# Numerators added by transfers, scores in four quarters, and GpSimd's arithmetic moved to VectorE and ScalarE, in a fused attention and feed-forward kernel

## The chip, the cores and the metric

The kernel runs on one core of a Trainium2 chip. The metric is the device time of one execution in microseconds (us). TensorE is called PE here, its weight load PEld, VectorE DVE, ScalarE ACT, GpSimd POOL, and SyncE, which issues the DMA transfers, SP, as the profile names them.

## What is computed

The reference, cut to what matters, with four batches, 8 heads, 576 positions, head size 64, window 64 (2304 tokens of 512 numbers in all):

```python
scores = q @ k.T / 8, masked to 0 <= i - j < 64
attn = softmax(scores);  x = attn @ v           # 2304 x 512
h = x @ w_in                                    # 2304 x 2048
P = a0 + a1*h + a2*h*h + a3*h*h*h
Q = 1 + |b0|*|h| + |b1|*h*h
x = (P / (Q + 1e-6)) @ w_out                    # 2304 x 512
out = ((x @ w1) * (x @ w2)) @ w3 @ wo2          # 2304 x 512
```

## The kernel before

All products of large matrices are made of three fp32r products of high and low parts (`TERMS`). Each weight tile is converted on DVE and ACT into such a pair (`conv`, lines 431 to 512: three shifts, a high part on ACT, a low part on DVE).

The 2304 tokens are cut into five blocks (`TOKENS`, line 30: two of 384, three of 512). A block has two units for the attention (`US`), of 3 windows of 64 queries (192 tokens) or 4 (256 tokens). A step is one unit and one pair of heads; there are 40 steps, treated in pairs (`attn`, lines 536 to 680). A step multiplies queries by keys into `sp` (`S_`, line 609), one window at a time: in the first four units (`THIN`) as two 64x64 products, one for each head, in the others as one 128x128 product with a query tile in which zeros keep the heads apart. Then follow the masked minimum on DVE (`tr`), the exponential on ACT (`e`), the sum plus 1e-9 on POOL (`rs`, line 557), its reciprocal on DVE (`rc`), the normalisation (`nm`, line 627: ACT, POOL or DVE, as the planner chooses), a transposition on PE (`T`), a copy on ACT (`ac`), and the product with the values (`O`). From step 24 on the probabilities go through a transfer within SBUF before the transposition (`mv`, tile `tq`). The output of the attention is split into the pair `xh`, `xl`.

The hidden layer (`chunks`, lines 685 to 829) takes two tiles of 128 of the 2048 hidden numbers at a time, called a pair here; a turn is one block and half of the hidden numbers, four pairs, and there are ten turns (`TURNS`, line 307): first blocks 0, 1, 2 with the first half, then 2, 1, 0 with the second, then 3, 4, 4, 3. For a pair PE computes `hp` (`H_`), ACT and DVE form the rational function, and PE multiplies the result `g` with `w_out` into `acc` (`D_`). The denominator is `Q`, `ln`, `ex`. The numerator comes in two ways. Where `estrin` holds (line 697, five of the ten turns), ACT makes a square `h2`, a linear term `u` and a second linear term `bl` from PSUM; DVE multiplies `u` by `h2` (`us`) and adds `bl` (`p`). In the other turns DVE reads PSUM four times for each pair (`uh`, `v`). Then DVE makes the high part of the quotient (`hi`), and by `w`, `d` and `lo` its low part. `lo` may run on DVE or POOL (line 818). The tiles `u`, `qa`, `g` have two buffers, `bl`, `h2`, `r` one.

After the hidden layer come the product of w3 and wo2 (`w_prod`, line 948), the two products of the second layer in Strassen's form (`p_`, line 1093), and the last product (`result`, line 1220).

The order of the instructions on every engine is fixed when the program is built: `Plan.order` (lines 97 to 241) books each operation with a duration on its engine, a tail (time until others may use its result) and a due time, walks through a list schedule with noise of a fixed seed on the due times, and the instructions are issued in that order. Engines take their queues in order and wait on semaphores.

Of the kernel before, what the change touches and what calls it, by code (L numbers as in the profile page):

```python
# [20 lines left out]
P = 128  # L21
# [8 lines left out]
TOKENS = (384, 384, 512, 512, 512)  # L30
# [7 lines left out]
NU = len(US)  # L38
NF = FF // P
# [26 lines left out]
class Plan:  # L66
# [30 lines left out]
    def order(self, rounds=16):  # L97
# [125 lines left out]
        rng = Random(67)  # L223
# [21 lines left out]
def body(ctx: ExitStack, tc: tile.TileContext, qkv, kv0, qk0, w_in, w_out, a, b, w1, w2, w3t, wo2, out):  # L245
# [21 lines left out]
    nc.gpsimd.memset(cq, QC)  # L267
    a0, a1, a2, a3 = (ca[:, i:i + 1] for i in range(4))
# [49 lines left out]
    MM = [{384: TMM, 512: TWM}[t] for t in TOKENS]  # L318
# [4 lines left out]
    TS, TT, TO, TOO = 0.67, 0.33, (0.71, 0.42), 1.9  # L323
# [25 lines left out]
    for t in range(-2 * NP - 1, NI + 1):  # L349
        scale[0] = 2.9 / (TS + TT + TO[0]) if t < 0 else 1.2 if t < 2 * NP * 2 else 1.0  # L350
# [185 lines left out]
    def attn(pair):  # L536
# [13 lines left out]

        def rows(f):
            return y["st"][:, 2 * NW * f:2 * NW * f + 2 * NW]
# [4 lines left out]
        def rs(_):  # L557
            nc.gpsimd.tensor_scalar(out=rows(2), in0=rows(1), scalar1=1e-9, scalar2=1.0, op0=ADD, op1=MUL)
# [4 lines left out]
        def O(k, y=y):  # L563
            if k == 0:
                y["op"] = psum.tile([P, 2, U], F32, tag="at", bufs=2, name="op")
            for w in range(NW):
                for h in (slice(0, 64), slice(64, P)):
                    nc.tensor.matmul(y["op"][h, k, w * W_:(w + 1) * W_], y["v", k][:, w, h], y["ac", k][:, w, h], start=True, stop=True)  # L568
            if u % 2 == 0 and k == 0 and y is units[u][0]:
                xh[j], xl[j] = xtiles(j, "x")  # L570

# [11 lines left out]
        def step(k):  # L583
# [5 lines left out]
            def load(_):  # L589
                x["k"] = ap_.tile([P, KB * W_], F32, tag="k", bufs=rings["k"], name="k")[:, 0:KU]  # L590
                if i < THIN:
                    if k == 0:
                        y["q"] = ap_.tile([P, 2 * UM], F32, tag="q", bufs=rings["q"], name="q")[:, 0:2 * U]
                        nc.sync.dma_start(out=y["q"], in_=qk0[u, p0 // 2])
                    x["q"] = y["q"].rearrange("d (k w n) -> d k w n", k=2, w=NW)[:, k]
                    nc.sync.dma_start(out=x["k"], in_=kv0[u, p, :, 0:KU])
                    return
                q = ap_.tile([P, 2 * UM], F32, tag="q", bufs=rings["q"], name="q")[:, 0:2 * U]
                x["q"] = q.rearrange("d (w n) -> d w n", w=NW)
                nc.sync.dma_start(out=q, in_=qkv[u - THIN // NP, p, :, 0:2 * U])  # L600
                nc.sync.dma_start(out=x["k"], in_=qkv[u - THIN // NP, p, :, 2 * U:2 * U + KU])

            def loadv(_):
                y["v", k] = ap_.tile([P, NWM, P], F32, tag="v", bufs=rings["v"], name="v")[:, 0:NW]
                v = kv0[u, p, :, U + W_:] if i < THIN else qkv[u - THIN // NP, p, :, 2 * U + KB * W_:]
# [3 lines left out]
            def S_(_):  # L609
                x["sp"] = sp = psum.tile([P, NW, P], F32, tag=tags[0], bufs=rings[tags[0]], name="sp")  # L610
                x["sm"] = ap_.tile([P, NWM, P], F32, tag="sm", bufs=rings["sm"], name="sm")[:, 0:NW]
                if k == 0:
                    y["st"] = ap_.tile([P, 8 * NWM], F32, tag="st", bufs=rings["st"], name="st")
# [38 lines left out]
            kb_, vb, qb, mb, sp, tp = ("k", i), ("v", i), ("q", i0 if i < THIN else i), ("sm", i), (tags[0], ("S", i)), (tags[1], ("T", i))  # L652
            thin = i < THIN
            op(("load", i), (("D", (0.48 if k else 1.12) if thin else 1.1 * wide),), load, after=[("load", i0)] if thin and k else (), new=(kb_,) if thin and k else (kb_, qb), uses=(qb,) if thin and k else (), tail=3.0)
            op(("loadv", i), (("D", 0.66 * wide),), loadv, after=(("load", i),), new=(vb,), tail=3.0)
            pe(("S", i), S_, TS * wide, after=[("load", i)] + [("S", i - 1)] * k, new=(sp, mb) if k else (sp, mb, sb), uses=(kb_, qb, sb) if k else (kb_, qb))
            for m in range(NW):
                op(("tr", i, m), (("V", 0.21),), lambda _, m=m: tr(m), after=(("S", i),), uses=(sp, mb, sb))
# [5 lines left out]
            pe(("T", i), T, 0.068 * NW if moved else TT * wide, after=[("mv", i)] if moved else [("nm", i)], new=(tp,), uses=(("tq", i),) if moved else (mb,))  # L664
# [6 lines left out]
        op(("rs", i0), (("P", 0.12),), rs, after=[("e", i0 + k, m) for k in range(2) for m in range(NW)], uses=(sb,))  # L671
# [686 lines left out]
```

## Time and profile before

| | before |
|---|---|
| median of 3 runs | 804.54 us (804.3 to 804.63) |
| profiled execution, device time | 805.03 us |
| its span | 803.3 us |
| PE busy | 782.0 us (97%) |
| PEld busy | 716.3 us (89%) |
| DVE busy | 729.7 us (91%) |
| ACT busy | 542.2 us (67%) |
| POOL busy | 50.5 us (6%) |
| DMA queue of SP | 168.85 MB, 60.5% of 16 engines' span |

The busy time of an engine is the time in which at least one of its instructions ran. Matmuls are pipelined and their ends are modelled, so that how many follow each other in a stretch says more than their durations.

### The profile page before, as it was taken

To read this page: it belongs to the slowest core of one execution; us is meant where nothing else is said; L and a number is where in the kernel's file an instruction comes from. 1 tells how busy PE (TensorE), PEld (TensorE's weight loads), DVE (VectorE), ACT (ScalarE), POOL (GpSimd) and SP (SyncE) were. 2 spreads that over 40 slices of the span, in tenths; PEclk is the share of its full clock that TensorE was granted. 3 is DMA by queue.
4 is the path that set the end of the run, shared out by engine and by line. 5 is a ranking of instruction groups with operands and counts; after the bars stand their busy time and mean duration, and the time that the engine had idled before them with its cause. 6 is when DMAs were issued, how large, how long until landed. Compare 5 with 4: busy or idle time off the path is not lost.

```text
span 803.3 us, 13413 instructions
## 1 busy us (share of the span) xinstructions
PE 782.0 (97%) x4728; PEld 716.3 (89%) x4728; DVE 729.7 (91%) x1361; ACT 542.2 (67%) x1131; POOL 50.5 (6%) x67
## 2 busy tenths in 40 slices
PE   5889999999999999999999999999999999999998
PEld 4679999888899999888888888889999999999998
DVE  6999999999999999999999999999998698847854
ACT  5888998859898988665677772377555447445434
POOL 1112112101100101200100000000000000000000
PEclk9899999999999999999999999999999999999999
DMA  8798884511657755537883365968898676136402
GB/s 292 249 334 305 293 278 157 186 54 65 207 185 282 273 191 203 202 133 236 323 282 143 117 221 183 313 249 292 307 305 282 210 283 195 42 133 222 145 1 78
DMA packets 66403, 169.70 MB, mean 211 GB/s; under 512 B 7456, under 2 KB 24864, under 8 KB 66336
## 3 DMA queue, kind: packets, MB, share of 16 engines
q1 hardware_dynamic: 66336, 168.85, 60.5%
q8 instruction: 37, 0.61, 0.3%
q14 instruction: 30, 0.25, 0.1%
HBM read 123.21 MB, written 41.42 MB: 205 GB/s over the span
## 4 chain that ended last, share of the span: by engine, by line
PE 83%; DVE 12%; DMA 2%; ACT 1%; issue 1%; POOL 0%; SPq 0%; POOLq 0%; DVEq 0%; ACTq 0%
PE acc L781 22%; PE hp L703 20%; PE pb L1093 9%; PE pa L1093 6%; PE pc L1093 6%; PE wp L948 5%; PE pb L1220 5%; PE pc L1220 3%; PE pa L1220 3%; PE sp L616 2%; DVE sm L619 2%; DVE wt L456 1%; DVE wt L453 1%; DVE wc L466 1%; PE op L568 1%; DMA cb<-in_b 1%
## 5 line engine op out<-in xcount | busy, mean ns | idle before, releaser
L703 PE MATMUL hp<-x,wc 128*128 128x512 f32 (+1 forms) x960 | 213.8, 371 | 3.6 <-DVE u L731 3.2
L781 PE MATMUL acc<-g,wc 128*128 128x512 f32 (+1 forms) x960 | 213.1, 370 | 0.0
L703 PEld LDWEIGHTS hp<-x,wc 128*128 128x128 f32 x960 | 173.7, 188 | 27.8 <-DVE u L731 4.2
L781 PEld LDWEIGHTS acc<-g,wc 128*128 128x128 f32 x960 | 173.9, 188 | 22.9 <-issue 0.3
L1093 PE MATMUL pb<-xb,wc 128*128 128x384 f32 x432 | 83.8, 334 | 0.0
L1093 PEld LDWEIGHTS pb<-xb,wc 128*128 128x128 f32 x432 | 75.7, 188 | 0.0
L744 ACT ACTIVATE r<-qa,cq 128x1024 f32<-128x1024 f32 (+1 forms) x40 | 42.8, 1069 | 37.8 <-DVE g L775 21.3
L625 ACT ACTIVATE sm<-sm,st 128x128 f32<-128x128 f32 x144 | 56.1, 395 | 17.3 <-DVE st L619 17.1
L720 ACT ACTIVATE qa<-hp,cb 128x512 f32<-128x512 f32 (+1 forms) x80 | 51.7, 647 | 19.3 <-PE hp L703 19.0
L725 ACT ACTIVATE u<-hp,ca 128x512 f32<-128x512 f32 (+1 forms) x80 | 59.5, 745 | 1.7 <-PE hp L703 1.3
L1093 PE MATMUL pa<-xb,wc 128*128 128x384 f32 x288 | 57.2, 335 | 0.0
L1182 ACT ACTIVATE rt<-prod 128x768 fp32r<-128x768 f32 x42 | 35.6, 847 | 31.9 <-PE pb L1220 13.3
L1093 PE MATMUL pc<-xb,wc 128*128 128x384 f32 x288 | 56.7, 334 | 0.0
L1185 DVE TENSOR_TENSOR rt<-prod,rt 128x768 fp32r<-128x768 f32 x42 | 40.1, 956 | 15.4 <-ACT rt L1182 14.9
L616 PE MATMUL sp<-k,q 64*64 64x128 f32 (+1 forms) x384 | 43.2, 311 | 10.2 <-DMA k<-in_kv 7.2
L463 ACT ACTIVATE wc<-wt 128x512 fp32r<-128x512 f32 x48 | 30.2, 633 | 32.7 <-DVE wt L456 29.0
L1093 PEld LDWEIGHTS pa<-xb,wc 128*128 128x128 f32 x288 | 50.6, 188 | 0.3 <-DMA wc<-kw 0.2
L453 DVE SCALAR_TENSOR_TENSOR wt<-ws,wt 128x512 uint32<-128x512 uint32 x72 | 50.4, 702 | 0.3
L1093 PEld LDWEIGHTS pc<-xb,wc 128*128 128x128 f32 x288 | 50.5, 188 | 0.0
L456 DVE SCALAR_TENSOR_TENSOR wt<-ws,wt 128x512 uint32<-128x512 uint32 x72 | 49.9, 695 | 0.3
L616 PEld LDWEIGHTS sp<-k,q 64*64 64x64 f32 (+1 forms) x384 | 37.9, 182 | 13.7 <-DMA k<-in_kv 4.0
L715 ACT ACTIVATE h<-hp 128x512 f32<-128x512 f32 (+1 forms) x80 | 44.3, 553 | 8.2 <-PE hp L703 7.1
(90 smaller groups left out, 1368.4 us busy)
## 6 DMA issues: line engine op xcount, KB each, us to landing
wc<-kw SPq DMA_DIRECT2D x48, 512.0 KB, 5.4
bs<-kb SPq DMA_DIRECT2D x24, 512.0 KB, 4.5
ws<-in_w_in SPq DMA_DIRECT2D x16, 512.0 KB, 6.1
ws<-in_w_out SPq DMA_DIRECT2D x16, 512.0 KB, 4.2
ws<-in_w SPq DMA_DIRECT2D x16, 512.0 KB, 4.3
kw<-ws SPq DMA_DIRECT2D x16, 512.0 KB, 3.5
ws<-in_w3t SPq DMA_DIRECT2D x16, 512.0 KB, 4.8
wsum<-wsum SPq DMA_DIRECT2D x16, 512.0 KB, 6.1
```

The lines of the kernel that those rows point to most:

```text
L453: stt(out=x["b"], in0=x["st"][:, :, 0], scalar=29, in1=x["b"], op0=ALU.logical_shift_right, op1=ALU.bitwise_or)
L456: stt(out=x["b"], in0=x["st"][:, :, 1], scalar=0xC0000000, in1=x["b"], op0=ALU.bitwise_and, op1=ALU.bitwise_or)
L616: nc.tensor.matmul(sp[h, w, :], x["q"][h, w], x["k"][h, kat[w] * W_:kat[w] * W_ + P], start=True, stop=True)
L625: act(x["sm"][:, m, :], x["sm"][:, m, :], AF.Exp, bias=col(0, k, m), scale=-1.0, accum_out=col(1, k, m))
L703: nc.tensor.matmul(x["hp", m], wf_(win, f0 + m)[:, s_, kk * P:(kk + 1) * P], (xh, xl)[m_][xk][:, kk, :], start=(kk == 0 and i == 0), stop= ...
L715: act(x["h2"][:, m, :], x["hp", m], AF.Square)
L720: act(x["qa"][:, m, :], x["hp", m], AF.Abs, scale=b0)
L725: act(x["u"][:, m, :], x["hp", m], AF.Identity, scale=a3, bias=a2)
L744: act(x["r"], x["qa"], AF.Ln, bias=cq)
L781: nc.tensor.matmul(accs[j, part, n], wf_(wout, f0 + m)[:, s_, n * P:(n + 1) * P], x["g"][:, m_, m, :], start=(first and i == 0), stop=(las ...
L1093: nc.tensor.matmul(x[m], sws[u, n, i0][:, s_, (c0 + k) * P:(c0 + k + 1) * P], t[:, m_, k, :], start=(first and k == 0 and i == 0), stop=(k ...
L1220: nc.tensor.matmul(x[m, n], w[:, s_, (c + n) * P:(c + n + 1) * P], rts[u, b, r][:, m_, k, :], start=(first and r == 0 and k == 0 and i == ...
```

## The change

- The order of the blocks becomes 384, 512, 384, 512, 512, and the pairs of steps stand at other places between the pairs of the hidden layer (`AT`).
- `S_` is one operation for both steps of a pair, in all units with 64x64 products: for each window, both steps and both heads. The first step writes head 0 to the upper half of its `sp` and head 1 to the lower, the second step the other way round, so the four products of a window and a pair use four different quarters of PE. `O` reads the halves of the second step swapped. It waits for both key tiles. The queries come without the zeros, one transfer for each pair of steps, in all units.
- `estrin` holds in all turns but the first. The addition `p` is a transfer within SBUF that adds its source `bl` to its target `u`, issued by POOL, booked as 1.5 us (at 384 tokens) on the DMA queue and a tail of 3.5.
- `rs` runs on DVE or ACT, `nm` on DVE or ACT, `lo` on DVE alone.
- Booked times, seed, and the due times of the first conversions change.

The diff, cut to its core:

```diff
-TOKENS = (384, 384, 512, 512, 512)
+TOKENS = (384, 512, 384, 512, 512)
...
+THINU = NU
...
-        rng = Random(67)
+        rng = Random(57)
...
+    tiny = pers.tile([P, 1], F32, name="tiny")
+    nc.gpsimd.memset(tiny, 1e-9)
...
-        AT[((-8, -6, -4, -2), (0, 1, 2, 3), (4, 5, 6, 6), (16, 18, 19, 20), (22, 24, 25, 26))[j][r // 2]].append(i)
+        AT[((-8, -6, -4, -2), (0, 1, 2, 2), (4, 5, 6, 6), (16, 18, 19, 20), (21, 23, 25, 26))[j][r // 2]].append(i)
...
-    TS, TT, TO, TOO = 0.67, 0.33, (0.71, 0.42), 1.9
+    TS, TT, TO, TOO = .72, 0.33, (0.71, 0.42), 1.9
...
-        if 0 <= i < NS:
+        if 0 <= i < NS and (what != "S" or i % 2 == 0):
...
-        scale[0] = 2.9 / (TS + TT + TO[0]) if t < 0 else 1.2 if t < 2 * NP * 2 else 1.0
+        scale[0] = 3.2 / (TS + TT + TO[0]) if t < 0 else 1.2 if t < 2 * NP * 2 else 1.0
...
-        def rs(_):
-            nc.gpsimd.tensor_scalar(out=rows(2), in0=rows(1), scalar1=1e-9, scalar2=1.0, op0=ADD, op1=MUL)
+        def rs(e):
+            if e == "A":
+                act(rows(2), rows(1), AF.Identity, bias=tiny)
+            else:
+                dve.tensor_scalar(out=rows(2), in0=rows(1), scalar1=1e-9, scalar2=1.0, op0=ADD, op1=MUL)
...
+        def S_(_):
+            for k in range(2):
+                y["place", k]()
+            y["st"] = ap_.tile([P, 8 * NWM], F32, tag="st", bufs=rings["st"], name="st")
+            for w in range(NW):
+                for k in range(2):
+                    for h in range(2):
+                        to = half[h if k == 0 else 1 - h]
+                        nc.tensor.matmul(y["sp", k][to, w, :], y["q", k][half[h], w], y["k", k][half[h], kat[w] * W_:kat[w] * W_ + P], start=True, stop=True)
...
-                for w in range(NW):
-                    for h in (slice(0, 64), slice(64, P)) if i < THIN else (slice(0, P),):
-                        nc.tensor.matmul(sp[h, w, :], x["q"][h, w], x["k"][h, kat[w] * W_:kat[w] * W_ + P], start=True, stop=True)
...
-            op(("nm", i), (("A", 0.32 * NW), ("P", 0.97 * wide), ("V", cost(0.065, 0.40))), nm, port=True, after=(("rc", i0),), uses=(sb, mb))
+            op(("nm", i), (("A", 0.32 * NW), ("V", cost(0.065, 0.40))), nm, port=True, after=(("rc", i0),), uses=(sb, mb))
...
-                op(("mv", i), (("D", 0.66 * wide),), mv, after=[("nm", i)], new=(("tq", i),), uses=(mb,), tail=3.0)
+                op(("mv", i), (("D", 0.66 * wide),), mv, after=[("nm", i)], new=(("tq", i),), uses=(mb,), tail=2.0)
...
-        op(("rs", i0), (("P", 0.12),), rs, after=[("e", i0 + k, m) for k in range(2) for m in range(NW)], uses=(sb,))
+        op(("rs", i0), (("V", 0.09), ("A", 0.2)), rs, after=[("e", i0 + k, m) for k in range(2) for m in range(NW)], uses=(sb,))
...
-        estrin = (j, f0 // HALF) in ((2, 1), (1, 1), (0, 1), (4, 0), (3, 0))
+        estrin = (j, f0 // HALF) in TURNS[1:]
...
         def p(_):
-            dve.tensor_tensor(out=x["u"], in0=x["u"], in1=x["bl"], op=ADD)
+            nc.gpsimd.dma_start(out=x["u"], in_=x["bl"], accum_op=ADD)
...
-            op(("p", c0), (("V", dve_(0.87, 2)),), p, port=True, after=(("us", c0), ("line", c1)), uses=(b["u"], b["bl"]))
+            op(("p", c0), (("D", 1.5 * T_ / 384),), p, tail=3.5, after=(("us", c0), ("line", c1)), uses=(b["u"], b["bl"]))
...
-            engines = (("V", dve_(0.87, 2)),) if whole else (("V", dve_(0.47)), ("P", 0.97 * T_ / 384))
+            engines = (("V", dve_(0.87, 2)),) if whole else (("V", dve_(0.47)),)
...
-    coming = {key: 3.2 * min(n, 12) + 8.5 * max(n - 12, 0) for n, key in enumerate(coming)}
+    coming = {key: 3.2 * min(n, 10) + 8.5 * max(n - 10, 0) for n, key in enumerate(coming)}
```

## Rows read from the trace of the kernel before

**Rows 1.** The page's part 1: busy us (share of span) xinstructions of each engine.

```profile
PE 782.0 (97%) x4728; PEld 716.3 (89%) x4728; DVE 729.7 (91%) x1361; ACT 542.2 (67%) x1131; POOL 50.5 (6%) x67
```

**Rows 2.** Stretches: length, busy of PE, PEld, DVE, ACT, POOL, PEclk, DMA, GB/s.

```profile
0.00:20.00 20.00, 10.64 (x88) 8.74 (x90) 13.70 (x54) 11.55 (x40) 3.37 (x15) 1.00 0.86 292
...
40.00:60.00 20.00, 16.07 (x161) 14.16 (x160) 19.64 (x55) 17.62 (x51) 2.33 (x3) 1.00 0.97 337
60.00:80.00 20.00, 20.00 (x179) 19.02 (x178) 19.79 (x50) 16.44 (x43) 5.01 (x6) 1.00 0.87 301
80.00:100.00 20.00, 20.00 (x162) 19.65 (x163) 20.00 (x55) 20.00 (x63) 2.55 (x5) 1.00 0.86 294
```

**Rows 3.** Timeline of PE, hidden layer at 512: start us, us, line, tile, count.

```profile
165.41 5.60 PE L703 MATMUL hp<-x,wc 128*128 128x512 f32 x24
170.85 4.92 PE L781 MATMUL acc<-g,wc 128*128 128x512 f32 x21
```

**Rows 4.** Timeline of PE around thin scores, value products, and wide scores.

```profile
64.69 1.53 PE L616 MATMUL sp<-k,q 64*64 64x128 f32 x24
66.15 2.36 PE L781 MATMUL acc<-g,wc 128*128 128x384 f32 x12
...
73.86 1.62 PE L568 MATMUL op<-sm,v 128*64 128x64 f32 x48
75.41 1.84 PE L781 MATMUL acc<-g,wc 128*128 128x384 f32 x9
...
255.11 1.95 PE L616 MATMUL sp<-k,q 128*128 128x128 f32 x16
256.82 1.81 PE L781 MATMUL acc<-g,wc 128*128 128x384 f32 x9
```

**Rows 5.** Groups by line and shape: count | busy us, mean ns | idle before, releaser.

```profile
L753 DVE TENSOR_TENSOR u<-u,bl 128x1024 f32<-128x1024 f32 x12 | 14.7, 1222 | 0.1
L753 DVE TENSOR_TENSOR u<-u,bl 128x768 f32<-128x768 f32 x8 | 7.6, 953 | 0.1
L728 DVE TENSOR_TENSOR u<-u,hp 128x512 f32<-128x512 f32 x24 | 15.9, 682 | 1.1 <-ACT u L725 0.9
L731 DVE SCALAR_TENSOR_TENSOR u<-u,ca,hp 128x512 f32<-128x512 f32 x24 | 17.4, 744 | 0.9 <-ACT qa L720 0.8
L775 POOL TENSOR_TENSOR g<-u,r 128x384 fp32r<-128x384 f32 x17 | 19.4, 1159 | 65.7 <-DVE u L770 30.9 <-ACT u L725 13.5 <-ACT sm L650 10.8
L775 POOL TENSOR_TENSOR g<-u,r 128x512 fp32r<-128x512 f32 x11 | 14.9, 1370 | 139.4 <-DVE u L768 59.6 <-PE hp L703 41.7 <-DVE u L770 38.0
L775 DVE TENSOR_TENSOR g<-u,r 128x512 fp32r<-128x512 f32 x37 | 25.0, 707 | 0.0
L736 ACT ACTIVATE bl<-hp,ca 128x512 f32<-128x512 f32 x24 | 19.4, 807 | 0.0
```

**Rows 6.** Timeline of DVE: multiplication and high part of one pair at 512.

```profile
184.03 1.22 DVE L750 TENSOR_TENSOR u<-u,h 128x1024 f32<-128x1024 f32 x1
...
187.50 1.22 DVE L759 TENSOR_TENSOR g<-u,r 128x1024 fp32r<-128x1024 f32 x1
```

**Rows 7.** DMA issues: count, KB each, median us from issue to landing.

```profile
ws<-in_w_in SPq DMA_DIRECT2D x16, 512.0 KB, 6.1
...
kw<-ws SPq DMA_DIRECT2D x16, 512.0 KB, 3.5
...
tq<-sm SPq DMA_DIRECT2D x16, 256.0 KB, 2.5
...
kb<-wt SPq DMA_DIRECT2D x16, 256.0 KB, 2.3
```

**Rows 8.** Groups by line: masked minima of the whole span; conversions up to 80 us.

```profile
L619 DVE CUSTOM_DVE_ANT_0 sm<-sp,mask 128x128 f32<-128x128 f32 x144 | 34.2, 285 | 2.5 <-PE sp L616 2.3
...
L456 DVE SCALAR_TENSOR_TENSOR wt<-ws,wt 128x512 uint32<-128x512 uint32 x14 | 10.1, 722 | 0.1
```

**Rows 9.** Instructions of GpSimd's two lines: count, ns min/median/max, first and last start.

```profile
L775 POOL TENSOR_TENSOR g<-u,r x28: 997/1274/2180, 53.7 to 394.8; 128x384 fp32r<-128x384 f32 x17, 128x512 fp32r<-128x512 f32 x11
...
L558 POOL TENSOR_SCALAR st<-st x20: 196/210/1238, 13.4 to 326.1; 128x8 f32<-128x8 f32 x12, 128x6 f32<-128x6 f32 x8
```

More of the change, by code (lines that the diff above doesn't have):

```diff
@@ L244, in body @@
 @with_exitstack
-def body(ctx: ExitStack, tc: tile.TileContext, qkv, kv0, qk0, w_in, w_out, a, b, w1, w2, w3t, wo2, out):
+def body(ctx: ExitStack, tc: tile.TileContext, kv0, qk0, w_in, w_out, a, b, w1, w2, w3t, wo2, out):
     nc = tc.nc
@@ L549, in attn @@
         y = units.setdefault(u, [{} for _ in range(NP // 2)])[p0 // 2]
+        half = (slice(0, 64), slice(64, P))
         def rows(f):
@@ L598, in load @@
[L598 to L601, printed above, removed]
+                if k == 0:
+                    y["q"] = ap_.tile([P, 2 * UM], F32, tag="q", bufs=rings["q"], name="q")[:, 0:2 * U]
+                    nc.sync.dma_start(out=y["q"].rearrange("d (k n) -> d k n", k=2), in_=qk0[u, p0 // 2].rearrange("d (k n) -> d k n", k=2)[:, :, 0:U])
@@ L603, in loadv, with place @@
+                y["q", k] = y["q"].rearrange("d (k w n) -> d k w n", k=2, w=NW)[:, k]
+                nc.sync.dma_start(out=x["k"], in_=kv0[u, p, :, 0:KU])
+                y["k", k] = x["k"]
             def loadv(_):
                 y["v", k] = ap_.tile([P, NWM, P], F32, tag="v", bufs=rings["v"], name="v")[:, 0:NW]
-                v = kv0[u, p, :, U + W_:] if i < THIN else qkv[u - THIN // NP, p, :, 2 * U + KB * W_:]
+                v = kv0[u, p, :, KU:KU + NW * P]
                 nc.sync.dma_start(out=y["v", k], in_=v.rearrange("r (w d) -> r w d", w=NW))
-            def S_(_):
-                x["sp"] = sp = psum.tile([P, NW, P], F32, tag=tags[0], bufs=rings[tags[0]], name="sp")
+            def place():
+                y["sp", k] = x["sp"] = psum.tile([P, NW, P], F32, tag=tags[0], bufs=rings[tags[0]], name="sp")
@@ L650, in ac @@
                 act(y["ac", k], x["tp"], cp)
-            kb_, vb, qb, mb, sp, tp = ("k", i), ("v", i), ("q", i0 if i < THIN else i), ("sm", i), (tags[0], ("S", i)), (tags[1], ("T", i))
-            thin = i < THIN
-            op(("load", i), (("D", (0.48 if k else 1.12) if thin else 1.1 * wide),), load, after=[("load", i0)] if thin and k else (), new=(kb_,) if thin and k else (kb_, qb), uses=(qb,) if thin and k else (), tail=3.0)
+            kb_, vb, qb, mb, sp, tp = ("k", i), ("v", i), ("q", i0), ("sm", i), (tags[0], ("S", i)), (tags[1], ("T", i))
@@ L655, in step @@
+            thin = True
+            op(("load", i), (("D", (0.48 if k else 1.12) * wide),), load, after=[("load", i0)] if thin and k else (), new=(kb_,) if thin and k else (kb_, qb), uses=(qb,) if thin and k else (), tail=3.0)
             op(("loadv", i), (("D", 0.66 * wide),), loadv, after=(("load", i),), new=(vb,), tail=3.0)
-            pe(("S", i), S_, TS * wide, after=[("load", i)] + [("S", i - 1)] * k, new=(sp, mb) if k else (sp, mb, sb), uses=(kb_, qb, sb) if k else (kb_, qb))
+            if k == 0:
+                sp1, mb1 = (f"acc{(i + 1) % 2}" if early else "at", ("S", i + 1)), ("sm", i + 1)
+                pe(("S", i), S_, TS * wide, after=[("load", i), ("load", i + 1)], new=(sp, mb, sb, sp1, mb1), uses=(kb_, qb, ("k", i + 1)))
@@ L661, in step @@
             moved = i >= MOVED
             if moved:
-                op(("mv", i), (("D", 0.66 * wide),), mv, after=[("nm", i)], new=(("tq", i),), uses=(mb,), tail=3.0)
-            pe(("T", i), T, 0.068 * NW if moved else TT * wide, after=[("mv", i)] if moved else [("nm", i)], new=(tp,), uses=(("tq", i),) if moved else (mb,))
+                op(("mv", i), (("D", 0.66 * wide),), mv, after=[("nm", i)], new=(("tq", i),), uses=(mb,), tail=2.0)
+            pe(("T", i), T, 0.075 * NW if moved else TT * wide, after=[("mv", i)] if moved else [("nm", i)], new=(tp,), uses=(("tq", i),) if moved else (mb,))
@@ L1322, in queries @@
         return out.reshape(NP, P, -1)
[L1324 to L1325 removed]
+    thin = range(THINU)
+    pad = lambda x: np.concatenate([x, np.zeros((NP, P, KB * W_ + NWM * P - x.shape[2]), x.dtype)], axis=2)
+    qk0 = np.stack([pad(queries(u, False))[:, :, :UM] for u in thin])
     return {
[L1327 to L1329 removed]
+        "kv0": np.stack([pad(np.concatenate([keys(u, len(blocks(u)[0])), values(u)], axis=2)) for u in thin]),
+        "qk0": qk0.reshape(THINU, NP // 2, 2, P, -1).transpose(0, 1, 3, 2, 4).reshape(THINU, NP // 2, P, -1),
         "w_in": cols(moe_w_in, NF),
```

24 lines of the change are left out of this document (6 added, 18 removed).

## The prediction

> **What bounds the kernel now.** I read four views in this order: the busy totals, the 20 us stretches, the order of TensorE's matmuls, and the groups by line and shape. The totals [rows 1] name TensorE (PE, 782.0 us of 803.3) with VectorE (DVE, 729.7) close behind. The stretches [rows 2] tell where each of them sets the pace. In the first 60 us PE is busy for 10.64 of 20 and still only 16.07 of 20 at 40 to 60, while DVE rises to 19.64: the start waits for DVE. From 60 us PE shows 20.00 of 20, and DVE 19.79 and 20.00 beside it. A busy PE need not be PE at its peak, so I checked the spacing: 24 hidden-layer matmuls of 512 columns fill 165.41 to 170.85, then the next run begins at once, 227 ns each [rows 3]. The engine is streaming. So past 60 us a microsecond of PE work removed is a microsecond gained, as long as DVE, which is as full, doesn't become later than PE; before 60 us only DVE work counts.
>
> The profiled execution took 805.03 us for its span of 803.3; the median of the runs is 804.54. I take the sum from 804.5, since all steps are differences.
>
> **Scores in quarters.** Before, a pair of thin steps (block of 384, 3 windows) issues 24 products 64x64, two side by side: 64.69 to 66.15 is 1.46 us, 61 ns each [rows 4]. A wide pair (block of 512, 4 windows) issues 16 full products: 255.11 to 256.82 is 1.71 us, 107 ns each [rows 4]. After, both kinds issue 64x64 products, 24 or 32 in a pair, on four quarters in turn. No row shows four quarters. Bounds for one product: 107/4 = 27 ns if they overlap fully, and 61 ns if only two overlap as in the thin row. The nearest row for many small products on PE is the value product: 48 of them from 73.86 to 75.41, 32 ns each [rows 4], where PE already swallows one weight load and one short product every 32 ns. I take 32. A thin pair becomes 24 x 0.0323 = 0.78 us (saves 0.68), a wide pair 32 x 0.0323 = 1.03 (saves 0.68). There are 8 thin and 12 wide pairs before and after. Four thin pairs, those of block 0, lie in the start, where PE waits anyway: worth 0. The rest: 16 x 0.68 = 10.9 us on the path. At 27 ns with all 20 counted it is 12 x 0.85 + 8 x 0.82 = 16.8; at 61 ns it is 12 x (1.71 - 1.95) = -2.9, a loss.
>
> The Trainium skill (TensorEngine Tiling (Array Packing), Restrictions and Gotchas) speaks against it: different row tiles must not write one PSUM bank at the same time. The rows disagree already: the thin products of the kernel before write both halves of one bank from two row halves, and take 61 ns each, where one alone takes the 107 of a 128-column product [rows 4]. By the rule two of them would have to take turns and the change would be worth nothing for thin pairs; I go by the rows.
>
> **DVE's load.** Turns with the split polynomial go from five to nine. The old ones were 12 pairs at 512 and 8 at 384; the new ones are 24 and 12. The addition leaves DVE in the old ones: 12 x 1.222 + 8 x 0.953 = 22.3 us [rows 5]. The 16 pairs that are new lose two products and two fused multiply-adds from PSUM, 2 x (0.682 + 0.744) = 2.85 at 512 [rows 5], and get one multiplication of 1.22 (same shape as the addition): 1.63 x 12 + three quarters of that x 4 = 24.5 us. Against that come 17 and 11 low parts from GpSimd [rows 5], at 0.707 and about 0.53 on DVE: 16.8 us; seven normalisations and twenty little sums are 7 x 0.6 + 20 x 0.2, some 8 us if none goes to ScalarE. Net: DVE is lighter by 22.3 + 24.5 - 16.8 - 8 = 22 us, all of it before 490 us. Since PE has no idle time there, this is worth 0 by itself. It is what lets DVE follow a PE that is 11 us faster, with 22 - 11 = 11 us over, 0.3 us for each of 36 pairs. ScalarE gets 24 and 8 more linear terms at 0.807 and about 0.6 [rows 5], 24 us; at 80 to 100 us it is full too (20.00, [rows 2]), so there the new load can cost a few us; elsewhere I cost it at nothing.
>
> **The adding transfer.** It stands between the multiplication and the high part, which now begins 2.25 us after the multiplication ends (185.25 to 187.50, [rows 6]). No row has an adding transfer or one that GpSimd issues. From below: 256 KB within SBUF land in 2.5 us, 512 KB take 3.5 against 2.3 for 256 KB to memory [rows 7], so 512 KB moved once are 3.7 us. From above: if the target is read too, 1024 KB, 6.1 us, and under load times 6.1/3.5 (the same size with the queue full, [rows 7]): 10.6. I take 6 for 512 KB, near the unloaded row counted twice. The code's planner books 1.5 + 3.5 = 5.0 at 384 tokens and 5.5 at 512, and orders DVE's queue by that; behind the waiting high part stand the next weight conversions and the next pair's denominator, and the output products wait for its low part. With 5.5 booked and 6 needed nothing is lost if DVE has other work in its queue, which its fullness says it mostly has: 0, at worst the rival below. On GpSimd's queue nothing else is left, so its waits hold up nobody. SP loses 12 query transfers of 256 KB.
>
> **The start.** DVE's list up to the end of the first turn (about 90 us) grows: eight low parts and four normalisations of that stretch came from GpSimd, 12 x 0.53 = 6.4; eight sums x 0.2 = 1.6; block 1 now has 4 windows instead of 3 in 8 steps, 8 masked minima x 0.24 [rows 8] = 1.9. Together 9.9 us if all is on the path. Nothing can be dropped: 14 of the 16 conversions that the first turn needs were done by 80 us [rows 8]. But the normalisations may go to ScalarE (2.1), DVE is no longer held by GpSimd (a low part of it takes 1.0 to 2.2 us for the same work, [rows 9]), DVE was idle for 6.3 us of the first 20 [rows 2], and past 60 us the next turn needs less DVE time. Between 0 and +9.9 I take +3.
>
> **Sum.** 804.5 - 10.9 + 3 = 796.6; I say 796.5.
>
> **Rivals.** (1) The transfer is late, slower than before. If it lands later than booked by more than the 0.3 us that DVE has left in a pair, DVE stands still at the high part 36 times, and each us is 36 us. At 1 us too late: 796.5 + 36 x 0.7 = 822. It decides at 0.3 + 8/36 = 0.5 us too late on average. For it: the upper bound of 10.6, and a GpSimd instruction of 0.21 us that once took 1.24 [rows 9], which an issue could suffer as well. Against: DVE's queue holds conversions between the two steps already now [rows 6], so a small delay is filled. The Trainium skill (SBUF — State Buffer, Who interferes with whom) says that GpSimd writes the descriptors of its transfers through the port pair that it shares with VectorE, and that an instruction in a two-port mode keeps it out, while a two-input product doesn't; no row here shows a descriptor written. By that rule only the short shifts (one input) could hold an issue, and the rival would be small.
> (2) Only two quarters overlap: 804.5 + 2.9 + 3 = 810.4. For it: no row has four. Against: 32 ns for the value products.
> (3) The start costs all of its 9.9: 803.5, next to nothing gained. For it: DVE's 19.64 at 40 to 60 us.
> (4) More than forecast: 27 ns, all pairs, no loss at the start: 804.5 - 16.8 = 787.7, and 785 if the earlier scores use DVE's idle time there.
>
> **How the numbers follow.** Forecast 0.60, (1) 0.16, (2) 0.06, (3) 0.10, (4) 0.08. About 0.2% (1.6 us) is what a measurement here can tell from no change; half of (3) falls within it. Faster 0.60 + 0.08 + 0.05 = 0.73, same 0.05, slower 0.22. The range goes from (4)'s 785 to 812, past (2) and a third of the way into (1); what it leaves out is most of (1) and little else.
>
> **What would show it.** Right: a run of 32 score products of a pair in about 1.0 us; PE at 20.00 from about 63 us; DVE near 707 us; the transfer landing in about 6 us with no idle time of DVE before the high part. Wrong: idle time of DVE put down to a DMA on the numerator's tile, PE waiting for low parts past 100 us, score products at 61 ns, or a first full PE stretch that comes at 70 us.

## The result, and the profile after

The changed kernel takes 814.41 us (median of 3 runs, 813.28 to 817.39) against 804.54: a ratio of 1.0131, 95% interval 1.0089 to 1.0173. It is slower, clear of the noise; 796.5 was forecast, and the time lies outside the range of 785 to 812. The profiled execution took 813.28 us, its span 811.5.

The page's part 1 after (busy us, share of the span, instructions), to be read beside [rows 1]:

```profile
PE 777.6 (96%) x4920; PEld 704.6 (87%) x4920; DVE 710.5 (88%) x1350; ACT 552.7 (68%) x1152; POOL 37.5 (5%) x49
```

DVE is 19 us lighter, PE 4.4, and yet the span is 8.2 us longer: both engines wait more. The first place is the start. Stretches (columns as in [rows 2]) of the changed kernel, the first three and one at the end of the hidden layer, and behind them the two of the kernel before that [rows 2] leave out:

```profile
0.00:20.00 20.00, 6.91 (x78) 5.27 (x82) 13.44 (x48) 10.08 (x35) 2.06 (x13) 1.00 0.81 273
20.00:40.00 20.00, 15.87 (x168) 12.38 (x160) 19.84 (x75) 16.00 (x56) 0.00 (x0) 0.91 0.81 278
40.00:60.00 20.00, 14.28 (x123) 13.03 (x124) 16.97 (x46) 17.15 (x54) 0.00 (x0) 0.83 0.84 294
...
480.00:500.00 20.00, 14.69 (x60) 11.76 (x58) 16.50 (x22) 6.46 (x10) 0.86 (x1) 0.91 0.64 216
```

```profile
20.00:40.00 20.00, 16.11 (x176) 12.91 (x173) 18.96 (x61) 16.21 (x58) 3.45 (x6) 0.83 0.76 250
...
480.00:500.00 20.00, 20.00 (x90) 16.57 (x89) 19.93 (x30) 6.93 (x10) 0.00 (x0) 1.00 0.49 174
```

PE is busy for 37.06 us of the first 60, where the kernel before has 10.64 + 16.11 + 16.07 = 42.82. At 480 us it is busy for 14.69 of 20, where it was for 20.00. What PE waited for (us in total, times, longest; "issue" is time in which it waited for nothing that the profile shows), and the waits of DVE and ACT that belong to the transfers (ACT must not overwrite `bl`, which has one buffer, before the transfer has read it):

```profile
PE sp L589 <- DMA k<-in_kv: 7.4, 2, 4.1
PE acc L794 <- DVE g L788: 5.3, 1, 5.3
...
PE hp L716 <- DVE x L600: 3.0, 1, 3.0
PE sp L589 <- issue: 2.9, 1, 2.9
PE hp L716 <- DVE u L744: 2.5, 1, 2.5
...
DVE g L772 <- DMA u<-bl: 9.3, 6, 3.2
...
ACT bl L749 <- DMA u<-bl: 5.7, 5, 2.3
```

Two things came as forecast. A pair of wide scores (timeline of PE: start, us, line, tile, count) starts at 48.66 and ends where the next run begins, at 49.69: 32 products in 1.03 us, 32 ns each, where [rows 4] have 1.71 us for the same scores. And the adding transfers (part 6: count, KB each, median us to landing) take the 5.5 that was estimated as 6:

```profile
48.66 1.10 PE L589 MATMUL sp<-k,q 64*64 64x128 f32 x32
49.69 2.35 PE L716 MATMUL hp<-x,wc 128*128 128x384 f32 x12
...
u<-bl POOLq DMA_DIRECT2D x24, 512.0 KB, 5.5
...
u<-bl POOLq DMA_DIRECT2D x12, 384.0 KB, 4.6
```

To see where time goes I use one figure more: PE's lost time, the length of a stretch less the matmuls that ran in it, each at its spacing in an unbroken run (227 ns at 512 columns as in [rows 3], 173 at 384; scores 107, 61 or 32 and value products 32 as in [rows 4] and above; transpositions 61 and 95). It is good to about 1 us, since records can be missing.

```
PE's lost time, us        0-60 us   60-560 us   median, us
before                      29.4        7.6      804.54
changed                     39.2       18.8      814.41
```

The quarters take 20 pairs x 0.68 = 13.6 us off the work. The lost time grew by 9.8 + 11.2 = 21.0. The difference, +7.4, is most of the 8.2 us by which the two profiled spans differ.

### The profile page after: what moved, and what is told of

The parts are those of the page before. It is cut to its first block, busy times and chain, and to the rows that moved or that the text cites. A ratio compares the mean times of both kernels' runs of the same rounds, so it can differ in the third digit from the quotient of the medians.

```text
span 811.5 us, 13799 instructions
## 1 busy us (share of the span) xinstructions
PE 777.6 (96%) x4920; PEld 704.6 (87%) x4920; DVE 710.5 (88%) x1350; ACT 552.7 (68%) x1152; POOL 37.5 (5%) x49
## 5 line engine op out<-in xcount | busy, mean ns | idle before, releaser
L716 PE MATMUL hp<-x,wc 128*128 128x512 f32 (+1 forms) x960 | 216.9, 376 | 6.5 <-DVE x L600 3.0
L716 PEld LDWEIGHTS hp<-x,wc 128*128 128x128 f32 x960 | 175.9, 191 | 32.2 <-DVE x L600 3.1
L749 ACT ACTIVATE bl<-hp,ca 128x512 f32<-128x512 f32 (+1 forms) x72 | 54.6, 759 | 5.7 <-DMA u<-bl 5.7
L772 DVE TENSOR_TENSOR g<-u,r 128x1024 fp32r<-128x1024 f32 (+1 forms) x36 | 40.8, 1134 | 19.8 <-DMA u<-bl 9.3
L1195 ACT ACTIVATE rt<-prod 128x768 fp32r<-128x768 f32 x42 | 35.5, 846 | 32.3 <-PE pb L1233 10.6
L766 POOL DMA_DIRECT2D u<-bl x36 | 35.4, 983 | 449.0 <-ACT sm L636 113.8
L456 DVE SCALAR_TENSOR_TENSOR wt<-ws,wt 128x512 uint32<-128x512 uint32 x72 | 49.2, 690 | 0.6
```

Of the source, the lines that this page charges most:

```text
L456: stt(out=x["b"], in0=x["st"][:, :, 0], scalar=29, in1=x["b"], op0=ALU.logical_shift_right, op1=ALU.bitwise_or)
L716: nc.tensor.matmul(x["hp", m], wf_(win, f0 + m)[:, s_, kk * P:(kk + 1) * P], (xh, xl)[m_][xk][:, kk, :], start=(kk == 0 and i == 0), stop= ...
L749: act(x["bl"][:, m], x["hp", m], AF.Identity, scale=a1, bias=a0)
L772: dve.tensor_tensor(out=x["g"][:, 0], in0=x["u"], in1=x["r"], op=MUL)
```

## The experiments

Letters: A, the transfers come late; B, the start is late because POOL's work went to DVE and ACT; M, joining two steps delays the start; K, the new sequence of the blocks delays it; P, the random draw of the planner decides. All ratios are to the kernel before on the same chip; it took 804.1 to 804.9 us on each of them, so that times of different experiments compare to about 1 us. "In the same order" means that every engine keeps its queue; "planned anew" means that the planner makes another order.

**e1, the transfers left out,** the changed kernel's order held. The numerators lack their linear part, so it shows time only.

```diff
-            nc.gpsimd.dma_start(out=x["u"], in_=x["bl"], accum_op=ADD)
+            pass
```

> The changed kernel in its own order of instructions, with the 36 adding transfers left out (the numerators lack their linear term). Theory A, the transfers land late and the waits behind them cost the time: the 5.3 us that PE stood still at 483 us, the slow clock behind that and the smaller losses between 60 and 490 us go, some 11 us, so about 803 us. Theory B, the loss is in the start, where VectorE took over GpSimd's work: the transfers begin only at 100 us, so 811 us or more stay.

Measured 804.61, ratio 0.9998 (0.9988 to 1.0007). In this order the transfers cost 9.8 us, 0.27 us for each of 36; the interval of the changed kernel's own ratio makes that good to some 3 us. PE's lost time from 60 to 560 us falls from 18.8 to 10.9, and the wait of 5.3 us shrinks:

```profile
PE acc L794 <- DVE g L788: 0.8, 1, 0.8
```

The start is still as bad (38.1 lost), and that eats what the quarters save: even with the transfers gone nothing is gained on the kernel before.

**e2, the additions on DVE,** in the same order.

```diff
-            nc.gpsimd.dma_start(out=x["u"], in_=x["bl"], accum_op=ADD)
+            dve.tensor_tensor(out=x["u"], in0=x["u"], in1=x["bl"], op=ADD)
```

> The changed kernel in its own order, with each addition as a VectorE instruction in the place where the transfer was issued. VectorE gets 24 x 1.222 + 12 x 0.953 = 40.8 us between 100 and 490 us and had about 29 us idle there. Theory A: the waits go and 12 us of VectorE come, so 812 to 818 us, near the changed kernel. Theory B, and the transfers cost nothing as they are: 826 us or more.

Measured 836.5 (1.0391, 1.0368 to 1.0413). DVE's busy time rises from 710.5 to 747.3, by 36.8 us, and the time by 22.1 over the changed kernel, 31.9 over e1: in this order most of what is added to DVE reaches the end.

**e3, two quarters,** in the same order: both steps of a pair on the two diagonal quarters.

```diff
-                        to = half[h if k == 0 else 1 - h]
+                        to = half[h]
```

> The changed kernel in its own order, with both steps of a pair on the same two diagonal quarters, so that only two products overlap. Wide pairs 32 x 0.061 = 1.95 us for 1.03, thin ones 1.46 for 0.82. If PE sets the pace past the start (both theories) the 9 wide and 4 thin pairs past 60 us cost 9 x 0.92 + 4 x 0.64 = 10.8 us: about 825 us. If the waits behind the transfers set the pace everywhere, PE's work hides in them: 814 to 818 us.

Measured 825.02 (1.0259, 1.0224 to 1.0293): 10.6 us over the changed kernel, near the 10.8 expected for 61 ns a product in place of 32: four quarters do overlap, and in an order that counts on them slower scores are paid in full. This is not the price of the change, which compares 32 products at 32 ns with 16 at 107; that both come to some 11 us is chance.

**e4, the start's small work back on POOL** (low parts of the first turn, the second step's normalisation in block 0, all sums), in the same order.

```diff
+                e = "P" if early and k == 1 else e
...
+            e = "P" if c0 < HALF else e
...
-            if e == "A":
-                act(rows(2), rows(1), AF.Identity, bias=tiny)
-            else:
-                dve.tensor_scalar(...)
+            nc.gpsimd.tensor_scalar(...)
```

> The changed kernel in its own order, with the low parts of the first turn, the second step's normalisation of the first four pairs and all little sums back on GpSimd. Theory B: the start gets back 3 to 6 us, 808 to 811 us. Theory A: within 2 us of the changed kernel's 814.

Measured 817.27 (1.0150, 1.0120 to 1.0179): no faster than the changed kernel, whose interval overlaps; PE is busy for 34.67 us of the first 60, less than the 37.06 there. B gets no support. It isn't refuted either, since a low part takes longer on POOL (1159 ns where DVE needs some 530, [rows 5] and the prediction), in an order made for DVE.

**e5 and e6, the quarters alone.** The kernel before with the scores of all pairs joined in four quarters (e5), and the same with block 0's steps left apart (e6); additions on DVE in five turns, blocks in the old sequence, seed 67, planned anew.

```diff
+        def S_(_):
+            for k in range(2):
+                y["place", k]()
...
+            for w in range(NW):
+                for k in range(2):
+                    for h in range(2):
+                        to = half[h if k == 0 else 1 - h]
+                        nc.tensor.matmul(y["sp", k][to, w, :], ...)
```

> The kernel before with the scores in quarters alone (both steps of a pair in one operation, queries without zeros, and the two booked times of the moved transposition that this order needs); blocks, additions and engines as before. PE's work is 13.6 us less; four thin pairs of block 0 and three of block 1 lie in the start. Theory M, joining two steps to one operation delays the chain of the start (the fourth high-low split of the output came at 43.3 us for 38.1): 804.5 - 13.6 + 4.6 hidden + 4 = 799 to 801 us. Theory K, the late start comes from the new order of the blocks: 794 to 796 us.

> As the one before, but the four pairs of the first block keep one operation for each step, so that the start runs as in the kernel before. Both theories: 12 x 0.68 + 4 x 0.65 = 10.8 us of PE's work less, 793 to 796 us. Theory M: 4 us or more below the kernel with all pairs joined; theory K: within 2 us of it.

Measured 810.16 (1.0074, 1.0055 to 1.0092) and 807.28 (1.0031, 1.0019 to 1.0042). Without any transfer and with DVE's old work, PE's 10.9 us still don't arrive. The 2.9 us between them speak for M, but are within what a draw does (below). K isn't needed for a late start: e5 keeps the old sequence of the blocks, and block 0 is late in it all the same (see e10).

**e7, the transfers alone:** the kernel before with its 20 additions as transfers, planned anew.

```diff
-            dve.tensor_tensor(out=x["u"], in0=x["u"], in1=x["bl"], op=ADD)
+            nc.gpsimd.dma_start(out=x["u"], in_=x["bl"], accum_op=ADD)
...
-            op(("p", c0), (("V", dve_(0.87, 2)),), p, port=True, ...)
+            op(("p", c0), (("D", 1.5 * T_ / 384),), p, tail=3.5, ...)
```

> The kernel before with the adding transfers alone, in its five turns with the split polynomial (20 transfers instead of 20 additions on VectorE). Theory A, late transfers cost time wherever the queue of DMA is busy and at the end of the hidden layer: VectorE loses 22 us of work and PE, which is full, gains nothing from that, so 805 to 811 us, with PE standing still at about 480 us. If VectorE's work were the bound: 795 us or less.

Measured 828.5 (1.0292, 1.0255 to 1.0329), 24 us slower, with DVE lighter by 13 us and idle at the same step:

```profile
DVE g L759 <- DMA u<-bl: 12.9, 7, 3.7
```

**e8, a longer tail:** the changed kernel with 6.5 us booked for the transfer in place of 3.5, planned anew.

```diff
-            op(("p", c0), (("D", 1.5 * T_ / 384),), p, tail=3.5, ...)
+            op(("p", c0), (("D", 1.5 * T_ / 384),), p, tail=6.5, ...)
```

> The changed kernel with the transfer booked 3 us longer (tail 6.5 us instead of 3.5), so that the order leaves it the time of its slowest landings (8 to 9 us). Theory A, the loss comes from landings later than booked: 806 to 810 us, with less idle time of VectorE behind transfers than the 9.3 us. If the time between the multiplication and the low part is itself too long for the buffers, whatever is booked: 814 us or more.

Measured 824.98 (1.0261, 1.0226 to 1.0296). No wait of DVE for a transfer is left in this trace, and the kernel is still slower: DVE now waits for ACT's first part of the numerator. Since the order is new, part of the 10.6 us over the changed kernel can be the draw's (below); a cure it is not.

```profile
DVE u L763 <- ACT u L738: 15.8, 14, 2.3
```

**e9, the last turn free:** 4 of the 36 transfers left out, the changed kernel's order held; that turn's numerators lack their linear part, so it shows time only.

```diff
+            if (j, f0 // HALF) != TURNS[-1]:
                 nc.gpsimd.dma_start(out=x["u"], in_=x["bl"], accum_op=ADD)
```

> The changed kernel in its own order of work, with the adding transfers left out in the last of its nine turns only (4 of 36; the numerators of that turn lack their linear part, so this run shows time only). Leaving all 36 out took 9.8 us off (e1_no_addition, 804.61). Theory C, the loss sits in one place, where TensorE waits 5.3 us for VectorE's product of the last turn and then runs a stretch of 24 output matmuls in 7.08 us in place of 5.44: the time falls by 6 to 8 us, to 806.5 to 808.5. Rival, the loss is spread evenly over the turns: 9.8 x 4/36 = 1.1 us, 813.3.

Measured 811.71 (1.0083, 1.0062 to 1.0104): 2.7 us gained of the 6 to 8 expected; 1.1 by an even spread. The two intervals overlap, so that this run doesn't tell the two apart. Of the wait of 5.3 us 2.0 stay without any transfer in that turn, and the 24 matmuls behind it are no faster than in the changed kernel (7.21 us to the start of the next run; 6.91 there, last section):

```profile
L795 PE MATMUL acc<-g,wc 128*128 128x512 f32 (+1 forms) x960 | 215.4, 373 | 2.0 <-DVE g L789 2.0
...
487.79 7.38 PE L795 MATMUL acc<-g,wc 128*128 128x512 f32 x24 [1.97 <-DVE g L789]
495.00 4.92 PE L962 MATMUL wp<-wc 128*128 128x512 f32 x21
```

**e10 and e12, block 0's steps apart in the changed kernel,** without (e10) and with (e12) the last turn's four additions back on DVE, the last two lines of the diff; both planned anew.

```diff
+            if early:
+                pe(("S", i), lambda _: S1(k), 0.67 * wide, ...)
-            if k == 0:
+            elif k == 0:
...
+            if (j, f0 // HALF) == TURNS[-1]:
+                op(("p", c0), (("V", dve_(0.87, 2)),), p, port=True, ...)
```

> The changed kernel with the score steps of the first two units parted again (one step for each head, two of the four quarters at a time), planned anew; everything else as changed. Theory M, joining makes the first scores wait for both heads' loads and takes about 3 us in the start, as between e5_quarters_alone (810.16) and e6_quarters_late (807.28): 811 to 812, and TensorE busy more in the first 60 us. Rival, the start is late for its VectorE steps and transfers, not for the joined steps: 813.5 to 815.

> As e10_steps_parted, and the four additions of the last turn back on VectorE (4 x about 1.2 us of its time), planned anew. Theories C and M together: 814.4 less 7 for the last turn less 3 for the start plus 0 to 5 for VectorE, 804.5 to 809.5. Rival, the loss moves to another turn when the last is mended: 811 to 815.

Measured 823.07 (1.0229, 1.0203 to 1.0254) and 806.16 (1.0015, 1.0000 to 1.0029). Theory M's small gain in e10 is a loss of 8.7, and an edit of four operations then takes 16.9 off. No cost of these four operations is of that size. The planned order itself had to be measured.

The traces tell more than these totals. M's delay is there: the fourth split of block 0's output on DVE (`x`), with which its attention ends, starts later wherever block 0's steps are joined, in every planned order, e10 and e12 among those apart (start, us, line; before, changed, e10):

```profile
38.11 0.51 DVE L581 TENSOR_TENSOR x<-op,x 128x384 fp32r<-128x384 f32 x1
...
43.27 0.56 DVE L600 TENSOR_TENSOR x<-op,x 128x384 fp32r<-128x384 f32 x1
...
40.86 0.55 DVE L609 TENSOR_TENSOR x<-op,x 128x384 fp32r<-128x384 f32 x1
```

```
apart    before 38.1   e6 39.0   e7 37.2   e10 40.9   e11 39.2   e12 40.3   e15 39.8
joined   changed 43.3  e5 41.6   e8 43.6   e13 42.6   e14 43.2
```

Joining delays block 0 by some 2.5 us (e5 less e6; the changed kernel's three draws less e10 and e12). The 1 to 2 us by which e10 and e12 are later than the old kernel's draws can be B, K or the draw. What e10 loses, it loses later: PE's lost time from 60 to 560 us is 31.5 there against 18.8. Its waits for the transfers are the largest of all:

```profile
DVE g L783 <- DMA u<-bl: 24.5, 11, 5.6
ACT bl L760 <- DMA u<-bl: 13.7, 10, 2.9
```

**e11 and e15, the kernel before with another draw; e13 and e14, the changed kernel with another draw.** Nothing but the start value is changed, so all instructions are the same.

```diff
-        rng = Random(67)
+        rng = Random(57)
```

> The kernel before with nothing but the start value of the planner's random draw changed (67 to 57, the value of the changed kernel), so that its instructions are the same and their order on the engines another. Theory P, the order before is a lucky draw, and any newly planned order loses some microseconds of what the quarters save: 808 to 813, VectorE busy the same 730 us within 2. Rival, the draw is worth nothing: 803.5 to 806, and the missing gain of e6_quarters_late (expected 794, came 807.3) is VectorE's as a second bound.

> The changed kernel with the planner's random draw started at 67 (the value of the kernel before) in place of 57; nothing else. Theory P, the draw decides some 10 us either way and 57 is a bad one for both kernels (e11_other_draw: 815.0 against 804.6): 800 to 808. Rival, the loss is the change's own (transfers late, joined steps) whatever the draw: 812 to 820.

> The changed kernel with the draw started at 58. Theory P: anywhere between 800 and 825, as the changed kernel's planned orders so far came to 814.4, 817.3, 823.1 and 825.0 with small edits each. Rival, the loss is the change's own and the draw adds little: 812 to 817.

> The kernel before with the draw started at 58. Theory P: 804 to 820, on the mean of the two draws near 810; its 804.6 under 67 is at the good end. Rival, 57 was an outlier: 803 to 807.

```
draw           67        57        58       mean
before       804.54    814.98    812.79    810.8
changed      819.52    814.41    811.03    815.0
PE's lost time, us (0-60 / 60-560)
before     29.4/7.6   32.7/12.4  30.6/13.8  30.9/11.3
changed    35.7/28.8  39.2/18.8  37.1/17.9  37.3/21.8
```

Intervals of the ratios: e11 1.0111 to 1.0145, e13 1.0166 to 1.0198, e14 1.0062 to 1.0099, e15 1.0078 to 1.0116. The draw alone moves the kernel before by 10.4 us, as much as the whole loss; 67 is its best of the three. Under 57 and 58 the two kernels can't be told apart (the changed one 0.6 and 1.8 us faster, with overlapping intervals), under 67 it is 15 us slower; but equal start values don't make equal orders, since the two kernels book different operations. From 20 to 60 us PE is no busier in the kernel before under 57 than in the changed kernel, with no change in it:

```profile
20.00:40.00 20.00, 14.18 (x166) 10.87 (x162) 19.93 (x69) 18.10 (x65) 3.77 (x5) 0.91 0.88 314
40.00:60.00 20.00, 13.62 (x142) 11.64 (x139) 19.14 (x53) 16.46 (x47) 3.23 (x5) 0.98 0.85 281
```

The means differ by 4.2 us with a scatter of some 5 in each row: three draws don't settle the change's sign on average. Its losses do stand out in every column: 6.4 us more in the start, 10.5 more after it, against 13.6 saved. The order also decides how long DVE and ACT wait for the transfers, and the slow orders of the changed kernel and its variants are those that wait longest (us, from the traces; e12 has 32 transfers). That these waits make the time was tested in one order alone (e1):

```
                           e12      e14     changed     e13      e10
DVE / ACT for u<-bl     9.8/1.6  5.7/1.6   9.3/5.7  20.1/6.6  24.5/13.7
median                   806.16   811.03    814.41    819.52    823.07
```

**e16, DVE relieved in the order before:** its 20 additions left out (numerators without their linear part: time only), order held.

```diff
-            dve.tensor_tensor(out=x["u"], in0=x["u"], in1=x["bl"], op=ADD)
+            pass
```

> The kernel before in its own order of work, its 20 additions of the numerator's halves on VectorE left out (those numerators lack their linear part, so this run shows time only): some 22 us less on VectorE, every other instruction and the order on each engine unchanged. The prediction's term, TensorE alone sets the end past the start and VectorE's relief is worth nothing: 803.5 to 805. Rival D, VectorE is a second bound that holds TensorE through the waits in the middle: 790 to 800.

Measured 804.76 (1.0001, 0.9992 to 1.0010), with DVE at 712.2 in place of 729.7:

```profile
PE 782.1 (97%) x4728; PEld 716.2 (89%) x4728; DVE 712.2 (89%) x1341; ACT 541.3 (67%) x1131; POOL 49.1 (6%) x67
```

DVE's relief is worth nothing there, as the prediction had it.

**e17, the quarters in the order before,** operation for operation; both steps of a pair at the place of the first. **e18, the same at the place of the second** step (`k == 1` in the diff), the first step's minima and exponentials moved back as far; one pair stays in its old form, and there the value products of one step read the other half of the probabilities, which changes values and not work.

```diff
+                if not early:
+                    if k == 0:
+                        for n in range(2):
+                            y["place", n]()
...
+                        for w in range(NW):
+                            for n in range(2):
+                                for h in range(2):
+                                    nc.tensor.matmul(y["sp", n][half[h ^ n], w, :], ...)
+                    return
```

> The kernel before in its own order of work, op for op, loads and VectorE's additions unchanged; only the scores of the 16 pairs after block 0 are done as 64x64 products in four quarters, both steps of a pair at the place of the first (block 0 keeps two quarters a step). TensorE saves 16 x some 0.65 = 10.4 us. Theory Q, the prediction's term, with e16_before_no_addition (VectorE holds nothing in this order): 793 to 796. Rival V, once TensorE is lighter VectorE or a buffer holds it and the saving goes into waits, as in e5_quarters_alone (810.2) and e6_quarters_late (807.3), which were planned anew: 801 to 805.

> As e17_quarters_own_order, but a pair's joined scores stand at the place of its second step (by then the first step's PSUM buffer has been free since its own place, so nothing new is waited for), the first step's minima and exponentials moved back by the same distance; 15 pairs joined, the one pair where this can't be ordered stays as before. Theory R, the loss of e17 is the place alone: the waits of TensorE at scores and value products after block 0 fall from 12.4 us to under 3, and the time to 804.6 less 15 x 0.65 = 795, with up to 4 for the later minima: 795 to 799. Rival V, with TensorE lighter something else holds it (VectorE at the first layer's and second layer's products): 802 to 808.

Measured 816.79 (1.0147, 1.0121 to 1.0172) and 811.98 (1.0112, 1.0095 to 1.0129). PE was to be lighter by 10 us of work, and the kernel is slower by 12 and by 8. The timeline of PE in e17 shows how:

```profile
78.34 1.27 PE L630 MATMUL sp<-k,q 64*64 64x128 f32 x32
79.54 1.83 PE L803 MATMUL acc<-g,wc 128*128 128x384 f32 x9
...
88.49 0.44 PE L630 MATMUL sp<-k,q 64*64 64x128 f32 x4
89.82 1.09 PE L630 MATMUL sp<-k,q 64*64 64x128 f32 x28 [0.89 <-ACT sm L672]
90.84 1.31 PE L803 MATMUL acc<-g,wc 128*128 128x384 f32 x6
...
216.51 1.15 PE L571 MATMUL op<-sm,v 128*64 128x64 f32 x32
220.58 1.15 PE L571 MATMUL op<-sm,v 128*64 128x64 f32 x32 [2.92 <-DVE x L584]
221.66 7.32 PE L803 MATMUL acc<-g,wc 128*128 128x512 f32 x24
```

After 4 products PE stands: the pair needs both buffers of the ring `at` at once, and the second is still being copied by ACT. The products are dearer too: 1.46 us without the wait here, 1.20 at 78.34, where the changed kernel takes 1.03; why isn't shown. All runs of scores, each up to the start of the next run and without waits inside, add up to 37.9 us before, 32.5 in e17, 31.4 in e18 and 24.6 in the changed kernel, so that PE is lighter by 5 and 6 us, not by 10. At 216 us the value products wait 2.92 us for a buffer; this happens twice. From 60 us on, scores and value products wait 10.3 us in e17 and 2.6 in e18, and others stand in their place (e18's waits of PE over the whole span, and of DVE for the sums that POOL makes):

```profile
PE hp L737 <- DVE u L765: 6.5, 5, 3.3
PE sp L642 <- DVE x L596: 2.5, 4, 1.3
PE op L583 <- ACT sm L684: 2.0, 1, 2.0
PE sp L642 <- ACT sm L684: 1.4, 2, 0.9
...
DVE st L575 <- POOL st L572: 5.4, 5, 2.1
```

Rival V's 802 to 808 is missed too, by 4 us. DVE now waits 5.4 us for POOL's sums (1.2 in the kernel before) while PE waits for DVE. Whether a DVE as much lighter as PE would let the quarters through in this order wasn't tried, nor what less work on PE is worth without the new demand on buffers. None of the eighteen kernels is faster than the one before.

## Why the prediction was wrong, point by point

- **What bounds the kernel: half right.** "A microsecond of PE work removed is a microsecond gained", as long as DVE doesn't become later, is the step on which the forecast stood. In the order before, 17.5 us off DVE gain 0 (e16), as the prediction said. The 5 to 6 us off PE in e17 and e18 gain nothing either, but there new waits for buffers stand against them, so that the step itself was not tested alone. In the changed kernel's order more work counts on both: 36.8 us more on DVE cost 31.9 (e2 on e1), slower scores cost 10.6 (e3). This fits two bounds, PE at 20.00 and DVE at 19.79 of 20 [rows 2], that wait for each other through an order made for particular durations. That shortening either one is worth nothing is shown for DVE alone.
- **Scores in quarters: price right, arrival wrong.** 32 ns a product were forecast and came (24 thin ones take 0.82 us in place of 0.78). Six of the twenty pairs run before 60 us, not four, so that 14 x 0.68 = 9.5 us lie behind the start for the 10.9 of the sum. What the sum left out is the joined step's demand, two buffers and both loads at one place: 2.5 us later for block 0, and the waits of e17. The rule that the prediction weighed against the change (the Trainium skill, TensorEngine Tiling (Array Packing), Restrictions and Gotchas: row tiles must not write one PSUM bank at once) is not what these rows show: both row halves write each step's `sp`, and 32 products still take 1.03 us.
- **DVE's load: size right** (710.5 against "near 707"), and worth 0 by itself (e16).
- **The adding transfer: the term that failed outright.** It was put at 0; in this order it costs 9.8 (e1). The landing was estimated well, 5.5 against 6, and rival (1) named the mechanism, but as a mean: it priced a transfer late on average and gave each pair the same 0.3 us of slack. The trace has few waits, long ones. Of 36, six make DVE wait, 9.3 us together, and five hold up ACT at `bl`, 5.7 us, which the prediction had not thought of; the worst is shown in the last section. In other orders DVE waits 5.7 to 24.5 us: the price belongs to the order, not to the transfer alone.
- **The start: sign right, mis-sized.** +3 was taken, bounds 0 to 9.9. PE's lost time there is 9.8 us higher (39.2 against 29.4), 6.4 as a mean over three draws, and some 4 us of it (6 pairs x 0.68) are scores that got shorter while PE waited anyway, so that the start cost +5.7. The cause that the prediction named, DVE's work moved from POOL, is not shown (e4). Joining the steps, which it didn't cost, delays block 0 by some 2.5 us where orders can be compared. The rest, and what that delay is worth at the end, stay open. "Before 60 us only DVE work counts" was read too narrowly: PE's largest wait there is for key tiles from DMA, 7.2 us before and 7.4 after.
- **The draw: not in the sum at all.** Planning anew is a part of the change, since its seed, costs and sequence of blocks are. It moved the kernel before by +10.4 and +8.2, so the forecast's sum started from the best of three draws, 6.3 us below their mean. Of the rise of 9.9 us that much can be the draw's. The range of 27 us had no term for it.
- **The terms side by side,** by the lost time of the two profiles: scores behind the start -9.5 for -10.9, start +5.7 for +3, waits behind the start +11.2 for 0, of which 7.9 go with the transfers (e1) and 3.3 stay without a named cause.

## To carry to other kernels

When a program plans its own order, time the old kernel under a few other draws before costing an edit: that spread, 10 us here, is the least that the range must hold. Test an edit in a held order, where a step's work can be left out or lengthened alone. Here, with two engines full at once, more work on either was paid nearly in full, and less work on VectorE gained nothing. For a long transfer in the chain ask what its latest landings hold up, not only its median.

## What the runs showed of the hardware

An adding transfer within SBUF issued by POOL takes 856 to 1215 ns of POOL for its issue, and lands 4.4 to 9.1 us after it (one line's instructions: count, ns min/median/max; then its landing):

```profile
L766 POOL DMA_DIRECT2D u<-bl x36: 856/878/1215, 100.2 to 486.4; - x36
...
DMA to landing us min/median/max: 4.4/5.3/9.1
```

Some other transfers were slower beside it. In the changed kernel's order with and without the adding transfers (changed, then e1), `kw<-ws` to memory and `tq<-sm` within SBUF:

```profile
kw<-ws SPq DMA_DIRECT2D x16, 512.0 KB, 5.0
...
tq<-sm SPq DMA_DIRECT2D x16, 256.0 KB, 3.9
...
kw<-ws SPq DMA_DIRECT2D x16, 512.0 KB, 3.1
...
tq<-sm SPq DMA_DIRECT2D x16, 256.0 KB, 2.5
```

The large loads hardly differ (`wc<-kw` 4.9 and 5.0 us). One late landing, in the timelines of POOL, DVE and PE:

```profile
473.02 0.87 POOL L766 DMA_DIRECT2D u<-bl  x1 [10.51 <-DVE g L788]
...
481.96 1.23 DVE L772 TENSOR_TENSOR g<-u,r 128x1024 fp32r<-128x1024 f32 x1 [3.24 <-DMA u<-bl]
...
488.78 7.08 PE L794 MATMUL acc<-g,wc 128*128 128x512 f32 x24 [5.31 <-DVE g L788]
```

The transfer is issued at 473.02 and the high part starts at 481.96, 8.9 us later, though 5.5 is the median. PE's wait of 5.3 us has a second cost: the 24 matmuls behind it take 6.91 us to the start of the next run at 495.69, where [rows 3] have 5.44 for the same work. The granted clock of that stretch is 0.79, so that part of it ran at 1.2 GHz in place of 2.4:

```profile
488.78:495.69 6.91, 6.91 (x24) 5.66 (x25) 5.37 (x8) 2.73 (x3) 0.00 (x0) 0.79 0.54 141
```

The same 24 matmuls behind other waits: 7.16 us behind 2.92 in e17 (clock 0.76), 7.21 behind 1.97 in e9 (0.76), and 5.57 behind 0.78 in e1 (1.00). Shortening the wait from 5.3 to 2.0 us didn't give the clock back.

In the changed kernel groups of four score products, one in each quarter, follow each other every 109 ns, where one whole 128x128 product of 128 columns takes 107 [rows 4]: the four overlap fully, and the rest of the 1.03 us is spent at the ends of the run.
